# Another order of the prologue's stages in an attention and feed-forward kernel on one core

## The chip, the cores and the metric

The kernel runs on one core of a Trainium2 chip. The core has a matrix engine (PE, TensorE), a vector engine (DVE), an activation engine (ACT), a general engine (POOL) and a sequencer that issues transfers (SP). Each executes its own instructions in order, and they wait for each other by semaphores. Transfers run on 16 DMA engines that all queues share. The metric is the time of one execution on the device in microseconds (us).

## The reference

Attention with two kinds of masks over 8 sequences of 576 tokens and 8 heads of 64, then a layer norm and a two-layer network (512 to 2048 to 512) with a residual:

```python
scores = scale * np.matmul(q, k.transpose(0, 1, 3, 2))
mask_local = (rel >= 0) & (rel < 32)                          # heads 0 to 3
mask_strided = (rel >= 0) & (pos[None, :] % 32 == pos[:, None] % 32)   # heads 4 to 7
scores = np.where(masks, scores, -1e9)
attn = np.exp(scores - np.max(scores, axis=-1, keepdims=True))
attn = attn / (np.sum(attn, axis=-1, keepdims=True) + 1e-09)
x = np.matmul(attn, v)                # heads side by side: (8, 576, 512)
xn = (x - mu) / np.sqrt(var + 1e-06) * g_ln
out = x + np.maximum(xn @ w_ch1, 0.0) @ w_ch2
```

## The kernel before

**Tiling.** Two heads make a *pair*; there are 32 pairs, four for each sequence, in the order strided, local, strided, local (heads 4 and 5, 0 and 1, 6 and 7, 2 and 3). The tokens of all sequences are cut into nine chunks of 512. For each chunk the network runs 16 steps, one for each 128 of the 2048 hidden units. The matrices of the network are each split in two parts of a rounded 32-bit format (high and low), and so are the inputs, so that a step takes 24 products of 128x128 by 128x512: eight of the high part of the first matrix (`ffn1_high`, L697), four of its low part (`ffn1_low`, L704), and twelve for the second layer (L724).

**Two regimes.** From chunk 1 on, the pieces of the attention for the next chunk stand at fixed places between the steps. Before that there is a prologue and chunk 0: the pairs 0 to 3 (sequence 0) must be through before chunk 0 can begin, pairs 4 to 8 are worked on between its steps, and the weights of each step come from HBM once and are split into their parts beside it. All of this is written as one list of words, `ORDER`. The program issues the words one after the other, and every engine keeps that order among its own instructions.

**The words.** `T:k:i:buf` turns the rows of q (i=0) or k (i=1) of pair k on PE, and `c:k:i` copies them on ACT. `S`, `mask`, `max`, `sub`, `exp`, `PP`, `pt`, `V`, `den`, `xo`, `X`, `xh`, `xl` carry pair k through scores (PE), mask and maximum (DVE), subtraction (POOL), exponential (ACT), turn (PE), copy (ACT), product with v (PE), division (DVE, two words), turn (PE), and the two parts of x (ACT, DVE). `vs` copies v once more on POOL (local pairs 1 and 3). `r` and `v` load a later pair, `st` stores a pair's result to DRAM (all SP); `tp` turns a loaded pair on DVE, out of a single buffer, so that the next `r` waits for it. For step f: `W:f` loads its two matrices of 512 KB (SP); for each matrix i, `low` (DVE) or `lowA` (ACT), `sc` (ACT), `mg` and `sg` (DVE) rebuild the numbers; `byg`, `add` (POOL), `cm` (PE), `cen` (DVE) multiply by the norm's weights and centre the first matrix; `hi` (ACT, L284) and `lo` (POOL, L288) write the two parts. `F:f`, `H:f`, `hh:f`, `hl:f`, `G:f` are the high and low products of the first layer (PE), the two parts of its result (ACT, DVE) and the second layer of step f (PE). `xr` reads a residual row block from DRAM (SP) and `xs` takes its mean and variance (DVE, POOL).

**Buffers that tie words together.** The last number of a PE word is one of three PSUM buffers; a word that writes a buffer waits until everything that reads the one before it is done. Buffers 1 and 2 become the second layer's sums with `G:0`, and after that only buffer 0 is left. The first layer has one buffer: `F:f` waits for `hl:f-1`. The numbers of one matrix pass through one PSUM buffer as well: `sc` of the next waits for `sg`. `W:10` takes memory that the pairs of sequence 0 used and so waits for `st:0` to `st:3`.

**Where chunk 0 ends.** `G:15` is issued inside chunk 1's first step, behind `ffn1(1, 0)`.

Of the kernel before, what the change touches and what calls it, by code (L numbers as in the profile page):

```python
# [17 lines left out]


ORDER = """  # L20
T:0:0:0 T:0:1:1 c:0:0: T:1:1:2 c:0:1: S:0::0 c:1:1: T:2:0:1 mask:0 max:0 T:1:0:2 c:2:0: sub:0
T:3:1:0 c:1:0: exp:0 S:1::1 PP:0::2 c:3:1: mask:1 pt:0 T:2:1:0 max:1 sub:1 V:0::1 c:2:1: T:3:0:2
den:0 vs:1 exp:1 xo:0 S:2::0 c:3:0: W:0 X:0::1 mask:2 vs:3 PP:1::2 xh:0 max:2 S:3::0 pt:1 xl:0
sub:2 r:4 V:1::2 mask:3 exp:2 low:0:0 sc:0:0 PP:2::1 max:3 pt:2 den:1 sub:3 mg:0:0 V:2::0 W:1 xo:1
exp:3 sg:0:0 X:1::1 tp:4 PP:3::2 sc:0:1 byg:0 xh:1 add:0 pt:3 v:5 V:3::2 den:2 low:0:1 low:1:0 W:2
mg:0:1 xo:2 low:1:1 cm:0::0 sg:0:1 cen:0 hi:0:1 v:4 xl:1 sc:1:0 S:4::0 lo:0:1 hi:0:0 den:3 mg:1:0
X:2::1 lowA:2:1 lo:0:0 mask:4 xh:2 W:3 sg:1:0 lowA:2:0 max:4 byg:1 sc:1:1 xo:3 sub:4 mg:1:1 X:3::0
add:1 xl:2 st:3 exp:4 xh:3 PP:4::2 W:4 sg:1:1 cm:1::1 lowA:3:0 xl:3 sc:2:0 cen:1 F:0 pt:4 mg:2:0
hi:1:0 sg:2:0 hi:1:1 lo:1:0 st:0 V:4::0 sc:2:1 lowA:3:1 H:0 mg:2:1 W:5 byg:2 lowA:4:0 den:4 lo:1:1
sg:2:1 hh:0 lowA:4:1 xo:4 add:2 sc:3:0 hl:0 X:4::0 hi:2:1 v:6 mg:3:0 F:1 xh:4 lo:2:1 sg:3:0  # L30
lowA:5:0 byg:3 xl:4 H:1 sc:3:1 st:2 G:0 lowA:5:1 mg:3:1 hh:1 sg:3:1 st:1 hl:1 sc:4:0 hi:3:1 r:5
mg:4:0 cm:2::0 lo:3:1 cen:2 sg:4:0 hi:2:0 add:3 sc:4:1 F:2 mg:4:1 lo:2:0 sg:4:1 W:6 cm:3::0 byg:4
cen:3 sc:5:0 H:2 hi:4:1 mg:5:0 G:1 add:4 hh:2 tp:5 hi:3:0 lo:4:1 st:4 sg:5:0 lo:3:0 hl:2 sc:5:1
cm:4::0 W:7 cen:4 lowA:6:0 F:3 byg:5 mg:5:1 lowA:6:1 hi:4:0 sg:5:1 add:5 S:5::0 sc:6:0 hi:5:1
lo:4:0 mg:6:0 r:6 H:3 mask:5 G:2 hh:3 lo:5:1 sg:6:0 lowA:7:0 hl:3 sc:6:1 byg:6 max:5 lowA:7:1
cm:5::0 mg:6:1 sub:5 W:8 F:4 cen:5 sg:6:1 add:6 hi:5:0 H:4 tp:6 exp:5 lo:5:0 sc:7:0 cm:6::0 G:3
hh:4 W:9 hi:6:1 mg:7:0 lo:6:1 lowA:8:0 hl:4 lowA:8:1 sg:7:0 F:5 cen:6 byg:7 sc:7:1 r:7 hi:6:0
mg:7:1 add:7 PP:5::0 sg:7:1 lowA:9:1 H:5 lo:6:0 sc:8:0 G:4 hh:5 mg:8:0 pt:5 hl:5 W:10 hi:7:1
sg:8:0 lowA:9:0 lo:7:1 cm:7::0 sc:8:1 F:6 tp:7 byg:8 cen:7 r:8 add:8 H:6 mg:8:1 hi:7:0 V:5::0
sg:8:1 hh:6 lo:7:0 lowA:10:0 hl:6 G:5 sc:9:0 den:5 xo:5 hi:8:1 lowA:10:1 lo:8:1 mg:9:0 W:11 sg:9:0  # L40
cm:8::0 F:7 cen:8 sc:9:1 byg:9 hi:8:0 mg:9:1 add:9 S:7::0 sg:9:1 st:5 sc:10:0 lo:8:0 H:7 mask:7
hi:9:1 W:12 G:6 mg:10:0 lowA:11:0 lo:9:1 max:7 hh:7 lowA:11:1 sg:10:0 sub:7 hl:7 sc:10:1 X:5::0
v:7 byg:10 exp:7 mg:10:1 F:8 xh:5 sg:10:1 lowA:12:1 xl:5 W:13 hi:10:1 H:8 sc:11:0 lo:10:1 cm:9::0
G:7 hh:8 cen:9 lowA:12:0 add:10 mg:11:0 hi:9:0 hl:8 W:14 lo:9:0 sg:11:0 cm:10::0 sc:11:1 F:9
cen:10 byg:11 lowA:13:1 mg:11:1 hi:10:0 add:11 sg:11:1 S:6::0 W:15 lowA:13:0 sc:12:0 lo:10:0 H:9
tp:8 hi:11:1 lowA:14:0 G:8 lo:11:1 hh:9 lowA:14:1 hl:9 r:9 mask:6 F:10 lowA:15:1 mg:12:0 lowA:15:0
max:6 cm:11::0 sg:12:0 sub:6 H:10 cen:11 sc:12:1 G:9 byg:12 hh:10 mg:12:1 exp:6 hl:10 add:12
hi:11:0 sg:12:1 tp:9 lo:11:0 sc:13:0 PP:6::0 hi:12:1 F:11 pt:6 mg:13:0 lo:12:1 r:10 sg:13:0
cm:12::0 H:11 sc:13:1 byg:13 cen:12 mg:13:1 V:6::0 hi:12:0 add:13 sg:13:1 hh:11 G:10 den:6 sc:14:0
lo:12:0 xr:0 hl:11 hi:13:1 mg:14:0 lo:13:1 v:8 xo:6 F:12 sg:14:0 xs:0 sc:14:1 byg:14 cm:13::0  # L50
mg:14:1 st:6 H:12 add:14 cen:13 G:11 hh:12 sg:14:1 hi:13:0 hl:12 sc:15:0 lo:13:0 hi:14:1 mg:15:0
cm:14::0 lo:14:1 sg:15:0 xr:1 F:13 cen:14 sc:15:1 byg:15 xr:2 hi:14:0 mg:15:1 PP:7::0 sg:15:1
lo:14:0 H:13 pt:7 xs:1 hi:15:1 X:6::0 add:15 xr:3 xs:2 hh:13 G:12 xh:6 lo:15:1 hl:13 xl:6 F:14
xs:3 cm:15::0 H:14 cen:15 V:7::0 hi:15:0 hh:14 lo:15:0 G:13 v:9 den:7 hl:14 xo:7 st:7 S:8::0 F:15
mask:8 tp:10 X:7::0 H:15 xh:7 max:8 G:14 hh:15 r:11 xl:7 sub:8 hl:15 exp:8 PP:8::0 pt:8
"""
# [904 lines left out]
```

## Time and profile before

| | |
|---|---|
| time, median of 3 runs | 949.44 us (947.91 to 950.6) |
| the profiled execution | 949.26 us, its span 946.7 us |
| PE busy | 915.5 us, 97% of the span |
| PE busy before 47.1 us | 31.3 us |
| PE busy from 59.9 to 165.3 us | 97.06 of 105.4 us |
| granted PE clock, mean | 0.986 |

The profile shows one execution. Times in it count from the span's start. An engine's idle time is put down to what ended it (the releaser); "issue" means that nothing shown ended it. Lines are those of the listing above.

### The profile page before, as it was taken

How to read it: one execution, taken by the hardware profiler on the slowest of the kernel's cores; microseconds unless marked ns; L12 is line 12 of the kernel's file. 1: busy time of each engine (PE TensorE's matmuls, PEld its weight loads, DVE VectorE, ACT ScalarE, POOL GpSimd, SP SyncE). 2: the span in 40 equal slices, each digit the busy share in tenths (PEclk: the TensorE clock that was granted, in tenths of full speed). 3: DMA queues.
4: the chain of work that ended last, by engine and by line, in shares of the span. 5: the costliest groups of instructions: out<-in, count | busy, mean ns of one | idle time of the engine just before them, and what ended most of it. 6: DMA issues, size and time to landing. Idle time of an engine off the chain costs nothing.

```text
span 946.7 us, 18534 instructions
## 1 busy us (share of the span) xinstructions
PE 915.5 (97%) x7840; PEld 755.2 (80%) x7840; DVE 405.8 (43%) x829; ACT 224.0 (24%) x361; POOL 147.5 (16%) x186
## 2 busy tenths in 40 slices
PE   7689889999999999999999999999999999999997
PEld 6567678888888888888888888888888888888886
DVE  3877676433543355334543344345433321122112
ACT  4576553211111111211111211121112111111110
POOL 5577654000100010001000010001000000000000
PEclk9799999999999999999999999999999999999999
DMA  9999953433433243423343344334221121002001
GB/s 188 222 240 220 272 104 73 106 63 72 89 87 64 50 95 60 97 44 84 62 97 62 86 73 97 62 86 74 72 38 49 36 86 38 1 1 89 1 1 44
DMA packets 239425, 80.14 MB, mean 85 GB/s; under 512 B 190064, under 2 KB 232688, under 8 KB 239344
## 3 DMA queue, kind: packets, MB, share of 16 engines
q1 hardware_dynamic: 236128, 77.27, 36.4%
q10 hardware_dynamic: 3216, 1.71, 0.8%
q8 instruction: 61, 1.00, 0.5%
q14 instruction: 20, 0.16, 0.1%
HBM read 59.48 MB, written 19.46 MB: 83 GB/s over the span
## 4 chain that ended last, share of the span: by engine, by line
PE 92%; issue 2%; DVE 2%; DMA 1%; POOL 1%; SPq 1%; ACT 0%; ACTq 0%; DVEq 0%; POOLq 0%
PE po L724 40%; PE ph L697 27%; PE ph L704 13%; PE m L505 2%; PE m L434 2%; PE n L490 1%; PE n L577 1%; DMA rows<-in_k_dram 1%; SPq L340 1%; PE av L505 1%; PE s L434 1%; PE pp L490 1%; PE cm L271 0%; PE t L360 0%; PE px L577 0%
## 5 line engine op out<-in xcount | busy, mean ns | idle before, releaser
L724 PE MATMUL po<-w,hh 128*128 128x512 f32 x1152 | 361.4, 395 | 0.0
L714 DVE SCALAR_TENSOR_TENSOR hl<-ph,hh 128x512 fp32r<-128x512 f32 x144 | 99.4, 690 | 461.5 <-ACT hh L709 461.1
L724 PEld LDWEIGHTS po<-w,hh 128*128 128x128 f32 x1152 | 211.9, 188 | 44.1
L697 PE MATMUL ph<-xh,w 128*128 128x512 f32 x576 | 228.1, 396 | 2.5 <-ACT w L284 1.4
L697 PE MATMUL ph<-xl,w 128*128 128x512 f32 x576 | 226.6, 393 | 0.0
L724 PE MATMUL po<-w,hl 128*128 128x512 f32 x576 | 224.9, 390 | 0.0
L709 ACT ACTIVATE hh<-ph 128x512 fp32r<-128x512 f32 x144 | 86.0, 597 | 489.7 <-PE ph L704 489.5
L704 PE MATMUL ph<-xh,w 128*128 128x512 f32 x576 | 155.4, 391 | 0.0
L697 PEld LDWEIGHTS ph<-xh,w 128*128 128x128 f32 x576 | 109.6, 190 | 25.8 <-ACT w L284 1.6
L697 PEld LDWEIGHTS ph<-xl,w 128*128 128x128 f32 x576 | 109.7, 191 | 22.6
L724 PEld LDWEIGHTS po<-w,hl 128*128 128x128 f32 x576 | 108.1, 188 | 23.2
L704 PEld LDWEIGHTS ph<-xh,w 128*128 128x128 f32 x576 | 107.2, 188 | 22.0
L480 POOL TENSOR_TENSOR sm<-sm,mx 128x648 f32<-128x648 f32 (+1 forms) x32 | 40.6, 1270 | 413.6 <-DVE mx L475 410.0
L674 POOL TENSOR_TENSOR rs<-rs,mhalf 128x1 f32<-128x1 f32 x36 | 19.8, 549 | 339.7 <-DVE rs L673 339.7
L486 ACT ACTIVATE sm<-sm 128x648 f32<-128x648 f32 (+1 forms) x32 | 23.8, 743 | 121.4 <-POOL sm L480 121.4
L288 POOL TENSOR_TENSOR w<-r,w 128x512 fp32r<-128x512 f32 x32 | 41.1, 1291 | 23.4 <-ACT w L284 19.4
L608 DVE TENSOR_TENSOR xl<-n,xh 128x480 fp32r<-128x480 f32 (+2 forms) x36 | 22.7, 660 | 15.5 <-ACT xh L604 15.5
L475 DVE TENSOR_REDUCE mx<-sm 128x12 f32<-128x648 f32 (+1 forms) x32 | 26.2, 820 | 2.5 <-DVE sm L469 0.5
L555 DVE TENSOR_TENSOR xo<-m,den 64x64 f32<-64x64 f32 (+3 forms) x120 | 27.1, 288 | 0.1
L248 DVE SCALAR_TENSOR_TENSOR p<-p,s 128x512 uint32<-128x512 uint32 x32 | 22.3, 696 | 10.5 <-ACT p L234 10.2
L669 DVE BATCH_NORM_STATS2 st<-x 128x6 f32<-128x512 f32 x36 | 24.3, 676 | 3.8 <-DMA x<-xds 3.8
L730 DVE SCALAR_TENSOR_TENSOR x<-po,rs,x 128x512 f32<-128x512 f32 x36 | 24.5, 736 | 3.1 <-PE po L724 2.8
(96 smaller groups left out, 599.7 us busy)
## 6 DMA issues: line engine op xcount, KB each, us to landing
s<-in_moe_w_ch_dram SPq DMA_DIRECT2D x32, 512.0 KB
out_dram<-x SPq DMA_DIRECT2D x32, 256.0 KB
raw<-in_q_dram SPq DMA_DIRECT2D x112, 72.0 KB
raw<-in_k_dram SPq DMA_DIRECT2D x112, 72.0 KB
xds<-xo SPq DMA_DIRECT2D x32, 162.0 KB
v_l<-in_v_dram SPq DMA_DIRECT2D x32, 144.0 KB
xdl<-xo SPq DMA_DIRECT2D x16, 256.0 KB
x<-xdl SPq DMA_DIRECT2D x32, 128.0 KB
```

Source lines behind the costliest of these rows:

```text
L288: nc.gpsimd.tensor_tensor(out=t[:, 1], in0=self.w[i], in1=t[:, 0].bitcast(F32), op=ALU.subtract)
L434: nc.tensor.matmul(o, lhsT, rhs, start=True, stop=True, tile_position=(64 * h, pos))
L475: nc.vector.reduce_max(mx[:, :, 0:nt], sm, axis=AX.X)
L480: nc.gpsimd.tensor_tensor(out=sm, in0=sm, in1=mx[:, :, 0:nt].unsqueeze(3).broadcast_to([P, 2, nt, sm.shape[3]]), op=ALU.subtract)
L505: nc.tensor.matmul(at(h, t)[cols], self.pt[rows, t, cols], self.v[rows, n, 0:w], start=True, stop=True, tile_position=(64 * h, cols.start))
L555: nc.vector.tensor_tensor(out=xo[r, t0:t1, h0:h1].rearrange("p t h d -> p h t d"), in0=av, in1=den[r, h0:h1, t0:t1].unsqueeze(3).broadcast_to(
L697: nc.tensor.matmul(ph, w1h[:, cc], x[:, cc, :], start=(cc == 0 and i == 0), stop=False)
L704: nc.tensor.matmul(ph, w1l[:, cc], xt[c][0][:, cc, :], start=False, stop=(cc == NCC - 1))
L709: nc.scalar.activation(out=hh, in_=ph, func=AF.Relu)
L714: nc.vector.scalar_tensor_tensor(out=hl, in0=ph, scalar=0.0, in1=hh.bitcast(F32), op0=ALU.max, op1=ALU.subtract)
L724: nc.tensor.matmul(po[i], hx[:, cs], w, start=(f == 0 and n == 0), stop=(f == NFC - 1 and n == 2))
L730: nc.vector.scalar_tensor_tensor(out=x, in0=po[i], scalar=rs, in1=x, op0=ALU.mult, op1=ALU.add)
```

## The change

`ORDER` has the same words, with other places and other PSUM buffers, and one word more, `Fb:0`: `F:0` now multiplies the first three pairs' part of x (six products) and `Fb:0` the fourth pair's (two). Every `F` goes over the parts of x in the order of the pairs, no longer by column. `BY_DVE` is empty and `ONCE` is false, so that the branches they stand in do what was done before.

```diff
-T:0:0:0 T:0:1:1 c:0:0: T:1:1:2 c:0:1: S:0::0 c:1:1: T:2:0:1 mask:0 max:0 T:1:0:2 c:2:0: sub:0
-T:3:1:0 c:1:0: exp:0 S:1::1 PP:0::2 c:3:1: mask:1 pt:0 T:2:1:0 max:1 sub:1 V:0::1 c:2:1: T:3:0:2
-den:0 vs:1 exp:1 xo:0 S:2::0 c:3:0: W:0 X:0::1 mask:2 vs:3 PP:1::2 xh:0 max:2 S:3::0 pt:1 xl:0
...
+T:0:1:0 T:0:0:2 c:0:1: T:1:1:1 c:0:0: c:1:1: S:0::0 T:2:1:2 mask:0 max:0 T:1:0:1 c:2:1: sub:0
+T:2:0:0 c:1:0: exp:0 S:1::2 c:2:0: PP:0::1 mask:1 T:3:1:0 pt:0 max:1 V:0::2 c:3:1: sub:1 S:2::1
+vs:3 vs:1 den:0 exp:1 xo:0 W:0 T:3:0:0 mask:2 X:0::2 c:3:0: max:2 PP:1::1 xh:0 sub:2 S:3::0 r:4
+pt:1 xl:0 low:0:0 sc:0:0 low:0:1 exp:2 mg:0:0 sg:0:0 V:1::1 mask:3 byg:0 W:1 PP:2::2 den:1 max:3
...
+BY_DVE = ()
+ONCE = False
+EARLY_F0 = True
...
-    def ffn1_high(c, f):
+    def ffn1_high(c, f, ccs=range(NCC), ph=None):
         xh, xl = xt[c]
-        ph = ps_h.tile([P, CH], F32, tag="h", name=f"ph{c}_{f}")
+        new = ph is None
+        if new:
+            ph = ps_h.tile([P, CH], F32, tag="h", name=f"ph{c}_{f}")
         w1h = w1s[f][:, 0].rearrange("p (c f) -> p c f", c=NCC)
-        for cc in range(NCC):
+        for n, cc in enumerate(ccs):
             for i, x in enumerate((xh, xl)):
                 nc.tensor.matmul(
-                    ph, w1h[:, cc], x[:, cc, :], start=(cc == 0 and i == 0), stop=False)
+                    ph, w1h[:, cc], x[:, cc, :], start=(new and n == 0 and i == 0), stop=False)
         return ph
...
-            p.load_v()
+            p.load_v(once=ONCE)
...
-            ph[k] = ffn1_high(0, k)
+            ccs = [p.h0 // 2 for p in first]
+            ph[k] = ffn1_high(0, k, ccs[0:-1] if EARLY_F0 and k == 0 else ccs)
+        elif op == "Fb":
+            ffn1_high(0, k, [first[-1].h0 // 2], ph[k])
```

The words of some engines, taken out of the two lists, each in its order. SP, all of its words up to the residual:

```
before  W0 r4 W1 v5 W2 v4 W3 st3 W4 st0 W5 v6 st2 st1 r5 W6 st4 W7 r6 W8 W9 r7 W10 r8 W11 st5 W12 v7
        W13 W14 W15 r9 r10 xr0 v8 st6 xr1 xr2 xr3 v9 st7 r11
after   W0 r4 W1 W2 r5 W3 v4 W4 W5 r6 W6 st3 W7 v5 W8 st0 W9 r7 st1 st4 st2 r8 W10 W11 W12 W13 W14
        st5 v6 W15 v8 st6 v7 r9 xr0 xr1 xr2 v9 xr3 r10 st7 r11
```

PE from pair 3's scores to the first second layer, and DVE from pair 0's `xl` to step 0's centring:

```
PE   before  S3 V1 PP2 V2 X1 PP3 V3 cm0 S4 X2 X3 PP4 cm1 F0 V4 H0 X4 F1 H1 G0
PE   after   S3 V1 PP2 V2 PP3 S4 X1 V3 X2 cm0 X3 PP4 F0 cm1 Fb0 H0 V4 S5 cm2 F1 H1 G0
DVE  before  xl0 mask3 low00 max3 den1 mg00 xo1 sg00 tp4 den2 low01 low10 mg01 xo2 low11 sg01 cen0
DVE  after   xl0 low00 low01 mg00 sg00 mask3 den1 max3 xo1 tp4 mg01 den2 sg01 mask4 low10 max4 mg10
             xo2 xl1 den3 xo3 sg10 cen0
```

ACT around step 8, and DVE at the end of the list:

```
ACT  before  hh7 lowA110 lowA111 sc101 exp7 xh5 lowA121 hi101 sc110 hh8 lowA120 hi90 ...
ACT  after   hh7 hi80 hi81 pt6 lowA100 sc100 lowA101 sc101 lowA110 hh8 sc110 hi90 lowA111 lowA121 ...
DVE  before  ... mg140 xo6 sg140 xs0 mg141 cen13 sg141 hl12 ... xs1 xs2 hl13 xl6 xs3 cen15 ... hl15
DVE  after   ... hl14 tp9 sg151 hl15 xl7 xs3 tp10 xs2 xs0 xs1
```

## Rows read from the trace of the kernel before

**Rows 1.** The page: busy time of the engines, and the granted clock.
```profile
PE 915.5 (97%) x7840; PEld 755.2 (80%) x7840; DVE 405.8 (43%) x829; ACT 224.0 (24%) x361; POOL 147.5 (16%) x186
...
PEclk9799999999999999999999999999999999999999
```
**Rows 2.** Windows by stage: length, busy PE, PEld, DVE, ACT, POOL, clock, DMA, GB/s.
```profile
0.00:47.10 47.10, 31.30 (x804) 27.23 (x805) 26.68 (x63) 23.96 (x34) 24.78 (x51) 0.85 0.96 205
...
59.90:165.30 105.40, 97.06 (x862) 77.43 (x861) 74.85 (x124) 55.31 (x94) 68.95 (x73) 0.97 0.73 174
```
**Rows 3.** What PE waited for, 59.9 to 165.3: total us, times, longest.
```profile
PE cm L271 <- POOL bsum L267: 5.4, 2, 2.9
PE ph L697 <- ACT w L284: 1.4, 1, 1.4
PE ph L697 <- DVE hl L714: 1.0, 1, 1.0
```
**Rows 4.** The chain that ended last, 100 to 143: start, us, what.
```profile
103.51 5.69 issue
...
112.58 3.12 PE ph L697 x8
...
126.78 1.85 PE ph L697 x8
...
133.49 5.32 issue
```
**Rows 5.** ACT in order of time, where it meets a weight transfer.
```profile
41.47 0.69 ACT L241 ACTIVATE s<-s 128x512 uint32<-128x512 uint8 x1 [1.58 <-DMA s<-in_moe_w_ch_dram]
...
107.97 0.67 ACT L241 ACTIVATE s<-s 128x512 uint32<-128x512 uint8 x1 [3.73 <-DMA s<-in_moe_w_ch_dram]
```
**Rows 6.** DVE in order of time, at `xs:0`.
```profile
137.66 0.69 DVE L669 BATCH_NORM_STATS2 st<-x 128x6 f32<-128x512 f32 x1 [3.82 <-DMA x<-xds]
```
**Rows 7.** DVE in order of time, at `mask:3` and `tp:4`.
```profile
27.80 0.82 DVE L462 TENSOR_TENSOR sm<-s,mask_l 128x640 f32<-128x640 f32 x1 [2.23 <-PE s L434]
...
31.97 1.25 DVE L409 STREAM_TRANSPOSE qt_s<-raw 128x576 f32<-128x576 f32 x1
```
**Rows 8.** DVE groups of the first 59.9 us: `mg` and `low`.
```profile
L248 DVE SCALAR_TENSOR_TENSOR p<-p,s 128x512 uint32<-128x512 uint32 x9 | 6.2, 694 | 1.8 <-ACT p L234 1.7
...
L244 DVE TENSOR_SCALAR s<-s 128x512 uint32<-128x512 uint32 x4 | 1.5, 388 | 0.0
```
**Rows 9.** Windows: GB/s moved (last column) while known transfers ran.
```profile
24.00:25.00 1.00, 0.45 (x41) 0.28 (x21) 0.94 (x2) 0.97 (x3) 0.94 (x2) 1.00 1.34 218
...
39.00:40.00 1.00, 0.72 (x28) 0.73 (x32) 0.97 (x4) 0.63 (x1) 0.70 (x2) 0.50 0.94 257
...
80.00:84.00 4.00, 3.02 (x15) 2.15 (x14) 2.95 (x5) 1.48 (x3) 1.86 (x3) 1.00 1.07 381
120.00:122.00 2.00, 2.00 (x10) 1.67 (x9) 2.00 (x4) 0.66 (x2) 0.40 (x1) 1.00 0.77 126
```
**Rows 10.** PE in order of time: V3, S4, X3, PP4, F0.
```profile
34.34 0.96 PE L505 MATMUL av<-v_l,pt 64*32 64x65 f32 x70 [0.84 <-ACT pt L495]
37.32 0.45 PE L505 MATMUL av<-v_l,pt 64*32 64x65 f32 x10 [2.03 <-issue]
...
39.28 1.54 PE L434 MATMUL s<-kt_s,qt_s 64*64 64x54 f32 x48 [0.78 <-DVE r L274]
...
43.93 1.09 PE L577 MATMUL px<-ident,xo 128*128 128x128 f32 x4 [1.64 <-DVE xo L555]
45.50 1.54 PE L490 MATMUL pp<-ident,sm 128*128 128x128 f32 x6 [0.48 <-ACT sm L486]
...
47.12 0.77 PE L697 MATMUL ph<-xh,w 128*128 128x512 f32 x1
```
**Rows 11.** PE in order of time: `G:0`, and the first product of chunk 1.
```profile
57.09 0.61 PE L724 MATMUL po<-w,hh 128*128 128x512 f32 x2
...
165.06 0.47 PE L697 MATMUL ph<-xh,w 128*128 128x512 f32 x1
```

More of the change, by code (lines that the diff above doesn't have):

```diff
@@ L20 @@
 ORDER = """
-T:0:0:0 T:0:1:1 c:0:0: T:1:1:2 c:0:1: S:0::0 c:1:1: T:2:0:1 mask:0 max:0 T:1:0:2 c:2:0: sub:0
-T:3:1:0 c:1:0: exp:0 S:1::1 PP:0::2 c:3:1: mask:1 pt:0 T:2:1:0 max:1 sub:1 V:0::1 c:2:1: T:3:0:2
-den:0 vs:1 exp:1 xo:0 S:2::0 c:3:0: W:0 X:0::1 mask:2 vs:3 PP:1::2 xh:0 max:2 S:3::0 pt:1 xl:0
-sub:2 r:4 V:1::2 mask:3 exp:2 low:0:0 sc:0:0 PP:2::1 max:3 pt:2 den:1 sub:3 mg:0:0 V:2::0 W:1 xo:1
-exp:3 sg:0:0 X:1::1 tp:4 PP:3::2 sc:0:1 byg:0 xh:1 add:0 pt:3 v:5 V:3::2 den:2 low:0:1 low:1:0 W:2
@@ L26 @@
[L26 to L55, printed above, removed]
@@ L56 @@
-"""
+T:0:1:0 T:0:0:2 c:0:1: T:1:1:1 c:0:0: c:1:1: S:0::0 T:2:1:2 mask:0 max:0 T:1:0:1 c:2:1: sub:0
+T:2:0:0 c:1:0: exp:0 S:1::2 c:2:0: PP:0::1 mask:1 T:3:1:0 pt:0 max:1 V:0::2 c:3:1: sub:1 S:2::1
+vs:3 vs:1 den:0 exp:1 xo:0 W:0 T:3:0:0 mask:2 X:0::2 c:3:0: max:2 PP:1::1 xh:0 sub:2 S:3::0 r:4
+pt:1 xl:0 low:0:0 sc:0:0 low:0:1 exp:2 mg:0:0 sg:0:0 V:1::1 mask:3 byg:0 W:1 PP:2::2 den:1 max:3
+sc:0:1 pt:2 xo:1 sub:3 V:2::2 tp:4 exp:3 W:2 PP:3::0 mg:0:1 pt:3 S:4::1 add:0 den:2 sg:0:1 r:5
+X:1::0 mask:4 sc:1:0 hi:0:1 low:1:0 V:3::1 max:4 lowA:2:0 xh:1 lo:0:1 mg:1:0 xo:2 sub:4 xl:1 W:3
@@ new lines @@
+exp:4 X:2::2 den:3 xo:3 lowA:2:1 cm:0::0 sg:1:0 xh:2 X:3::1 cen:0 byg:1 xl:2 hi:0:0 PP:4::0 v:4
+sc:1:1 lo:0:0 low:1:1 mg:1:1 xh:3 F:0 pt:4 add:1 sg:1:1 xl:3 sc:2:0 W:4 hi:1:1 lowA:3:1 mg:2:0
+cm:1::0 cen:1 Fb:0 sg:2:0 lowA:3:0 H:0 byg:2 sc:2:1 tp:5 add:2 W:5 V:4::0 hh:0 hi:1:0 mg:2:1
+S:5::1 lo:1:0 hl:0 sg:2:1 hi:2:1 cm:2::2 lo:1:1 F:1 cen:2 sc:3:0 r:6 mask:5 lowA:4:1 hi:2:0 H:1
+G:0 mg:3:0 sg:3:0 hh:1 den:4 lo:2:0 byg:3 sc:3:1 hl:1 lowA:4:0 W:6 lowA:5:0 mg:3:1 sg:3:1 F:2 H:2
+add:3 xo:4 sc:4:0 hi:3:1 mg:4:0 lowA:5:1 lo:3:1 sg:4:0 cm:3::0 st:3 G:1 cen:3 sc:4:1 byg:4 hi:3:0
@@ new lines @@
+W:7 hh:2 mg:4:1 sg:4:1 hl:2 sc:5:0 X:4::0 lo:3:0 mg:5:0 F:3 H:3 xh:4 sg:5:0 lo:2:1 add:4 v:5 xl:4
+byg:5 hi:4:1 sc:5:1 mg:5:1 lowA:6:0 cm:4::0 G:2 add:5 cen:4 hh:3 sg:5:1 hi:4:0 hl:3 sc:6:0 lo:4:0
+max:5 W:8 hi:5:1 cm:5::0 lowA:6:1 lowA:7:1 mg:6:0 sub:5 cen:5 sg:6:0 exp:5 F:4 H:4 tp:6 byg:6
+PP:5::0 st:0 hh:4 G:3 pt:5 add:6 W:9 hl:4 hi:5:0 sc:6:1 lo:4:1 lowA:7:0 mg:6:1 cm:6::0 lo:5:0
+sg:6:1 F:5 cen:6 sc:7:0 r:7 hi:6:0 mg:7:0 S:6::0 lowA:8:0 lo:6:0 sg:7:0 H:5 mask:6 sc:7:1 byg:7
+add:7 G:4 mg:7:1 hh:5 lowA:8:1 sg:7:1 hl:5 sc:8:0 st:1 lo:5:1 max:6 lowA:9:0 cm:7::0 mg:8:0 st:4
@@ new lines @@
+st:2 sub:6 cen:7 tp:7 hi:7:0 F:6 H:6 lo:7:0 V:5::0 hh:6 sg:8:0 r:8 hl:6 hi:7:1 sc:8:1 byg:8 G:5
+lowA:9:1 den:5 add:8 exp:6 mg:8:1 sg:8:1 sc:9:0 xo:5 F:7 hi:6:1 mg:9:0 lo:6:1 lo:7:1 W:10 sg:9:0
+cm:8::0 H:7 cen:8 sc:9:1 mg:9:1 PP:6::0 hh:7 G:6 sg:9:1 hi:8:0 hi:8:1 hl:7 lo:8:0 byg:9 pt:6 tp:8
+lo:8:1 lowA:10:0 F:8 sc:10:0 add:9 lowA:10:1 mg:10:0 W:11 W:12 S:8::0 sg:10:0 sc:10:1 H:8 mask:8
+byg:10 lowA:11:0 mg:10:1 cm:9::0 hh:8 G:7 add:10 sg:10:1 cen:9 sc:11:0 hl:8 hi:9:0 lowA:11:1
+lo:9:0 cm:10::0 F:9 lowA:12:1 mg:11:0 sg:11:0 cen:10 sc:11:1 byg:11 W:13 W:14 lowA:12:0 hi:10:0
@@ new lines @@
+S:7::0 mg:11:1 sg:11:1 add:11 H:9 mask:7 sc:12:0 lo:10:0 G:8 hi:9:1 mg:12:0 sg:12:0 hh:9 hl:9
+sc:12:1 byg:12 lowA:13:0 cm:11::0 mg:12:1 F:10 add:12 lowA:14:1 cen:11 st:5 v:6 sg:12:1 lo:9:1
+cm:12::0 sc:13:0 W:15 H:10 cen:12 hi:11:0 max:7 X:5::0 hi:10:1 G:9 mg:13:0 xh:5 lo:10:1 hh:10
+hi:11:1 sg:13:0 xl:5 lo:11:0 lowA:14:0 hl:10 V:6::0 hi:12:1 lowA:13:1 F:11 lo:12:1 v:8 den:6
+sc:13:1 xo:6 byg:13 lo:11:1 X:6::0 mg:13:1 sg:13:1 add:13 H:11 xh:6 st:6 G:10 sc:14:0 xl:6 hh:11
+v:7 sub:7 hi:12:0 hl:11 cm:13::0 lo:12:0 exp:7 F:12 cen:13 hi:13:1 hi:13:0 lowA:15:0 lo:13:1
@@ new lines @@
+mg:14:0 sg:14:0 byg:14 H:12 PP:7::0 r:9 max:8 sub:8 sc:14:1 mg:14:1 G:11 sg:14:1 lo:13:0 pt:7
+hh:12 hl:12 lowA:15:1 V:7::0 xr:0 exp:8 sc:15:0 add:14 mg:15:0 F:13 den:7 xo:7 sg:15:0 H:13 xr:1
+hh:13 byg:15 cm:14::0 add:15 G:12 cen:14 hi:14:0 sc:15:1 lo:14:0 xr:2 hi:14:1 hl:13 PP:8::0
+mg:15:1 F:14 pt:8 lo:14:1 v:9 cm:15::0 H:14 cen:15 G:13 hi:15:0 hh:14 hl:14 lo:15:0 tp:9 sg:15:1
+F:15 xr:3 H:15 X:7::0 hh:15 hi:15:1 hl:15 r:10 st:7 xh:7 lo:15:1 xl:7 xs:3 G:14 tp:10 xs:2 xs:0
+r:11 xs:1
+"""
+BY_DVE = ()
@@ L752 @@
     for p in first:
-        p.load_rows(0, nc.sync)
-        p.load_rows(1, nc.scalar)
+        if p.k in BY_DVE:
+            p.load_qk(early.tile([P, 2 * S], F32, name=f"raw{p.id}"))
+        else:
+            p.load_rows(0, nc.sync)
+            p.load_rows(1, nc.scalar)
     nc.scalar.dma_start(gcol, g_ln.rearrange("(c p) -> p c", p=P))
```

## The prediction

> **What bounds the kernel now.** I read the page first: PE is busy 915.5 of 946.7 us, so nothing but PE's idle time and its clock can be won, and the granted clock is below full only at the left end of the line [rows 1]. The windows by stage say where: 15.8 us of idle in the first 47.1 us at a mean clock of 0.85, and 8.3 us between 59.9 and 165.3 [rows 2]. Behind that PE has no gap. So the change is judged by two times alone: the start of `G:0`, and the first product of chunk 1, at 57.09 and 165.06 [rows 11]. Next I read what PE waited for in the second stretch: 5.4 us in two waits of `cm` for POOL, and two small ones of 1.4 and 1.0 [rows 3]. The releaser named there is not the cause. The chain shows before each of the two long waits a hole of over 5 us in which no engine of the chain worked [rows 4]; the engines' own rows fill them. At 107.97 ACT ends a wait of 3.73 us for a weight transfer (`lowA:12:1`), with `hi` and `hh` words behind it, for which POOL and then `cm` wait [rows 5]. At 137.66 DVE ends a wait of 3.82 us for a residual row block (`xs:0`), with `sg:14:0` and so `byg` and `cm` behind it in time [rows 6]. After each the clock is low for a while: the eight products of an `F` take 3.12 us where they take 1.85 at full speed [rows 4].
>
> **First stage, up to `F:0`.** Here I follow two engines.
>
> *DVE up to `tp:4`.* Before, DVE is idle 2.23 us until `mask:3` at 27.80, and then works without a break to `tp:4` at 31.97 [rows 7]. Four weight words of step 0 (`low`, `low`, `mg`, `sg`) now stand ahead of `mask:3`: 2 x 0.39 and, with `sg` taken like `mg`, 2 x 0.69 [rows 8], 2.2 us in all, which just fit the idle time. But `low:0:1` waits in order for W0's second matrix. The rate of a weight transfer is 381 GB/s and that of the small pieces of `r` 126 [rows 9]; the 218 of 24 to 25 us is then a mixture with 0.36 of the weights in it, so W0's last byte moved at 24.4. How long until DVE may use it? W2's last bytes moved at about 40.0, where the rate falls from 257, and ACT's wait for it ended at 41.47 [rows 5, 9]: 1.4 us. So `low:0:1` runs at 25.8, `mg` and `sg` end at 27.5, and `mask:3` starts there. Of the 4.17 us that follow, two `mg`/`sg` (1.4) and one `low` (0.4) have gone ahead, yet `max:3`, `den:1` and `xo:1` keep their order, and the two last wait for V1, which waits for the same fetch pause of PE as before; I count the work as 2.9 instead of 2.4 for that. `tp:4` starts at 30.4, 1.6 us earlier. Bounds: 2.2 us (no wait for W0) and 0 (W0 usable only at 27.4, 3 us after its last byte).
>
> The Trainium skill, page "DMA: Bandwidth & Descriptors", section "Anatomy of one DMA", puts the fixed cost of a transfer at about 2.0 us, most of it the confirmation of the last write, for transfers issued on POOL's path. SP's transfer above shows 1.4. By the page's figure `low:0:1` would run 0.6 us later and the sum below would be 9.5 instead of 10.1.
>
> *PE from V3 to `F:0`.* Before, V3 ends at 37.77 (with a fetch pause of 2.03 us in it) and `F:0` starts at 47.12: 9.35 us [rows 10]. In them lie S4 (0.78 wait, 1.54 work), waits of 1.64 before X3 and 0.48 before PP4, and `cm:1`. S4 now goes ahead, into buffer 1, and does not wait for `cen:0` any more: `tp:4` takes two transposes of 1.25, so S4 runs at 32.9 to 34.5. V3 needs its buffer, so `mask:4`; ahead of that DVE has `mg:0:1`, `den:2`, `sg:0:1`, which end at 34.6, and `mask:4` at 35.4. V3 begins at 35.4 instead of 34.34 and, with the same pause (the words ahead of it hold as many products as before, but for S4, X1 and `cm`), ends at 38.9. Behind it X2 1.5, `cm:0` 0.6, X3 1.1, PP4 1.5 at the low clock [rows 10] make 4.8: `F:0` at 43.7. X3 needs `xo:3`: DVE has seven words from 35.4 on, at 0.4 to 1.0 us each, and is there at about 40.2, before PE is. `xl:3` no longer holds `F:0`, as only `Fb:0` needs it. From `F:0` to `G:0` I take the 9.97 us of before [rows 10, 11]: S5 (1 us) comes in, X4 with its wait goes out. **Gain 3.4 us**, bounds 0 (DVE at its late bound, and the pause twice as long) and 5.5 (pause gone).
>
> The first words of the list (k before q, pair 2 before pair 3) I cost at nothing: S0 needs both copies of pair 0 in either order. `Fb:0` is two of the same eight products; the other order over x, `BY_DVE` and `ONCE` change no work.
>
> **Second stage, `G:0` to chunk 1.** PE's work is the same (X4 in, S5 out, 0.2 us). What can go is 8.3 us of idle [rows 2] and the slow clock behind the two long waits, twice 3.12 - 1.85, 2.5 us [rows 4].
>
> *The wait at `xs:0`.* All `xs` now stand behind `hl:15`, with no weight word behind them. The 2.5 us of PE's wait and the 1.3 of clock go. What is late next: `tp:10` and three `xs`, then chunk 1's first `hl`. `tp:10` waits for `r:10`, which now waits for `tp:9`; 0.59 MB at 126 GB/s are 4.7 us, and 1.4. From `tp:9`, about 9 us before chunk 1 (F15, H15, X7, G14 and part of G13), `r:10` lands 3 us before chunk 1 begins, `tp:10` and `xs` take 6: they end 3 us into it, where `hl` is due in 3.4 and only missed after another 4.7 (the pieces of pair 8 and `G:15` stand ahead of the next `F`). Covered.
>
> *The wait for W12.* Ahead of W12 the queue now lacks v6 (0.3 MB, 2.4 us) and st5 (0.32 MB, 0.9 to 2.6 us) [rows 9]: it lands at 103 to 104.7 instead of 107.97. `lowA:12:1` now stands behind `F:9` and behind `hh:8`. `F:9` ran at 112.2 before; less the 3.4 and the 2.9 of this very wait it runs at 105.9, and at 103 if the small waits go too. So the margin is between +2 and -1.7. I charge 1.2 us.
>
> W6 to W9 come earlier (v5, v6 and st0 to st2 stand behind them, r6 ahead: some 6 us at the rates of rows 9), W10 2.3 us later (r8 ahead of it, v6 no more).
>
> *Small waits.* 1.4, 1.0 and 0.5 (the rest of 8.3) belong to `hi`, to `hl` and to fetching; in a list as dense I expect as many again: 2.9 stay. DVE, busy 74.85 of 105.4 us [rows 2], would be at 79% of 95: not a bound, but no slack for many waits.
>
> **Sum**: 3.4 + 8.3 + 2.5 - 1.2 - 2.9 = **10.1 us**. The profiled execution took 949.26 us, within 0.02% of the median 949.44, so 939.2.
>
> **Rivals.**
>
> *The new wait* (22%): one of the long waits lives on at another place. W10 to W14 stand in one block behind `r:8`, which waits for `tp:7` and so for `r:7` to land; ACT meets them at `lowA:10:0`, `11:0`, `12:1`, with `hh:8`, `hi:9:0`, `hi:10:0` behind. For it: the queue moves 174 GB/s over the whole stretch [rows 2], between the rates of its two kinds, so it is hardly ever empty. Against it: the place of `lowA:12:1`. One episode costs what it did before, 2.9 and 1.3 us less the 1.2 charged: 942 to 945.
>
> *No small waits either* (10%): 10.1 + 2.9 + 1.2, 935.
>
> *Given back* (9%): the prologue's lead is lost to fetch pauses or to W0, and the seam to chunk 1 takes the rest: DVE ends `xs` not 3 but 15 us into chunk 1 because `r:10` lands late. Then 949. Against it: `r:10` has nothing big ahead of it.
>
> *Slower* (10%): the block W10 to W14 late as a whole. ACT then waits in order at each of its five places, and each is an episode of 2.9 + 1.3 = 4.2 us. Three eat the gain (12.6 against 10.1); from the fourth on the kernel is slower by more than 0.3%: 939.2 - 1.2 + 4 x 4.2 = 954.8. For it: `r:8` is issued only when DVE has done `tp:7`, in order behind `cen:7` and so behind PE. Against it: `tp:7` stands before `F:6`, some 13 us before `lowA:10:0`, and `r:8` with W10 takes 7.5.
>
> **Chances.** Likeliest 49%, its own range 936 to 942. 0.3% (2.8 us) is about what a measurement of this kernel can tell from no change. Faster: 49 + 22 + 10 and a point of the given back, 82%; the same 8%; slower 10%. The range runs from 932.5 (no waits, the fetch pause gone) to 947.5, which leaves out most of the two last rivals.
>
> **What would show it.** Right: `G:0` near 53.7 and chunk 1 near 155; ACT's waits for weights short; no wait of DVE for x before `hl:15`; clock full from `G:0` on; the rest of the span equal. Wrong: `mask:3` not before 27.8, a wait of `F` or `cm` over 2 us, or `hl` of chunk 1 held by `tp:10`.

## The result, and the profile after

The changed kernel takes **935.7 us**, the median of 4 runs (933.98 to 937.52), the kernel before 950.02 beside it (4 runs, 947.91 to 953.22): a ratio of 0.9847, with a 95% interval of 0.981 to 0.9883. The forecast was 939.2 in a range from 932.5 to 947.5. The profiled execution took 933.98 us, its span is 932.1.

The two times by which the change was to be judged cut the span into three stages. In the first row stands what [rows 1, 2, 11] give, with the span:

| | `G:0` | `G:0` to chunk 1 | chunk 1 to the end | span |
|---|---|---|---|---|
| before | 57.09 | 107.97 | 781.64 | 946.7 |
| after | 54.49 | 94.46 | 783.15 | 932.1 |
| won | 2.6 | 13.5 | -1.5 | 14.6 |
| forecast | 3.4 | 6.7 | 0 | 10.1 |

The page of the kernel after, the lines of [rows 1]:

```profile
PE 910.5 (98%) x7840; PEld 752.3 (81%) x7840; DVE 409.6 (44%) x829; ACT 223.3 (24%) x361; POOL 148.0 (16%) x186
...
PEclk9799999999999999999999999999999999999999
```

Its windows by stage (length, busy PE, PEld, DVE, ACT, POOL, clock, DMA, GB/s), which answer to [rows 2]:

```profile
0.00:54.50 54.50, 40.28 (x959) 34.29 (x960) 37.47 (x76) 29.74 (x44) 29.83 (x57) 0.87 0.94 214
54.50:148.95 94.45, 94.45 (x798) 76.67 (x796) 72.99 (x115) 60.32 (x103) 69.25 (x71) 1.00 0.82 201
148.95:932.10 783.15, 775.73 (x6087) 641.32 (x6085) 299.15 (x639) 133.25 (x214) 48.95 (x59) 1.00 0.29 63
```

The same windows of the kernel before, cut at its own times:

```profile
0.00:57.10 57.10, 40.32 (x883) 34.14 (x884) 34.48 (x76) 32.35 (x49) 31.53 (x58) 0.85 0.95 216
57.10:165.10 108.00, 99.67 (x874) 79.56 (x872) 77.51 (x129) 57.46 (x98) 69.19 (x74) 0.97 0.73 175
165.10:946.70 781.60, 775.56 (x6088) 641.52 (x6086) 293.81 (x626) 134.16 (x215) 46.76 (x55) 1.00 0.29 63
```

The middle rows hold the result. PE is busy for 94.45 us of 94.45: it waits for nothing in the whole second stage, where it had 8.33 us of idle time. Its granted clock is 1.00 in the mean (0.97 before) and its busy time is itself 5.2 us shorter. About 0.5 us of that is work that crossed the cut and is no gain: S5 (0.97 us) and `cm:2` (0.14) now stand ahead of `G:0`, X4 (0.58) behind it. Like for like the first stage won 3.1 us and the second 13.0. The products that change most are those of `F`, which stand behind the waits of before (groups of PE in the second stage, by line; count, busy us and mean ns of one, idle time before them), before:

```profile
L697 PE MATMUL ph<-xh,w 128*128 128x512 f32 x57 | 25.0, 439 | 2.5 <-ACT w L284 1.4 <-DVE hl L714 1.0
L697 PE MATMUL ph<-xl,w 128*128 128x512 f32 x56 | 23.5, 419 | 0.0
```

and after:

```profile
L704 PE MATMUL ph<-xh,w 128*128 128x512 f32 x57 | 23.2, 407 | 0.0
L704 PE MATMUL ph<-xl,w 128*128 128x512 f32 x56 | 21.9, 391 | 0.0
```

As many products take 3.4 us less. PE in order of time, at `F:0`, `G:0`, chunk 1's first product and the one wait behind it:

```profile
43.80 0.78 PE L704 MATMUL ph<-xh,w 128*128 128x512 f32 x1
...
54.49 0.61 PE L731 MATMUL po<-w,hh 128*128 128x512 f32 x2
...
148.95 0.39 PE L704 MATMUL ph<-xh,w 128*128 128x512 f32 x1
...
160.65 0.70 PE L731 MATMUL po<-w,hh 128*128 128x512 f32 x2 [1.41 <-DVE x L737]
```

What ACT waited for in the second stage (us in total, times, longest), its weight words and its `hh` words, before and then after:

```profile
ACT s L241 <- DMA s<-in_moe_w_ch_dram: 13.7, 10, 3.7
...
ACT hh L709 <- PE ph L704: 4.3, 5, 2.1
```
```profile
ACT hh L716 <- PE ph L711: 13.3, 9, 4.6
...
ACT s L246 <- issue: 0.8, 1, 0.8
```

ACT's idle time has changed its owner. Before, it waited ten times for a weight transfer, and its work was late; now its longest total is for PE, and no wait is put down to a weight (one of 0.8 us at a weight word has no releaser that the profile shows). An engine that waits for the one that sets the end has time in hand. ACT's waits for DVE's `r` fell as well, from 21.1 us to 12.7.

### The profile page after: what moved, and what is told of

It is laid out like the page before. It is cut to its first block, busy times and chain, and to the rows that moved or that the text cites. A ratio compares the mean times of both kernels' runs of the same rounds, so it can differ in the third digit from the quotient of the medians.

```text
span 932.1 us, 18549 instructions
## 1 busy us (share of the span) xinstructions
PE 910.5 (98%) x7840; PEld 752.3 (81%) x7840; DVE 409.6 (44%) x829; ACT 223.3 (24%) x361; POOL 148.0 (16%) x186
## 4 chain that ended last, share of the span: by engine, by line
PE 94%; DVE 2%; issue 1%; POOL 1%; DMA 1%; ACT 0%; SPq 0%; DVEq 0%; POOLq 0%; ACTq 0%
PE po L731 42%; PE ph L704 28%; PE ph L711 14%; PE m L510 2%; PE m L439 2%; PE n L495 1%; PE n L582 1%; PE t L365 1%; PE s L439 1%; DMA rows<-in_k_dram 1%; SPq L345 0%; PE pp L495 0%; POOL sm L485 0%; PE av L510 0%; PE cm L276 0%
## 5 line engine op out<-in xcount | busy, mean ns | idle before, releaser
L737 DVE SCALAR_TENSOR_TENSOR x<-po,rs,x 128x512 f32<-128x512 f32 x36 | 24.6, 740 | 3.1 <-PE po L731 2.8
```

What stands on the lines that cost most here:

```text
L737: nc.vector.scalar_tensor_tensor(out=x, in0=po[i], scalar=rs, in1=x, op0=ALU.mult, op1=ALU.add)
```

## Experiments

Times of one profiled execution stand with every kernel, cut at the same two points; that execution is the slowest run of y1, y3 and y7 and the fastest of x2. (The 97.3 us that the expectations of y4, y5 and y6 name for the second stage, and the 105 of x5, are counted 2.8 us further, to the end of chunk 1's first `F` and `H`.) Two things are read off this table before any single row: the second stage is 94.4 to 94.6 us in seven kernels with the new order, and the first stage moves by 4.1 us between two kernels whose words before `G:0` are the same (the changed kernel and y1). The kernel before stood at 950.02 beside the changed kernel (4 runs) but at 947.81 to 948.91 in the three larger groups of the table (53 runs), so that the gain is probably nearer 12 to 13 us than the 14.3 between those two medians.

| kernel | `G:0` | `G:0` to chunk 1 | rest | median us (runs) | before beside it | ratio, 95% interval |
|---|---|---|---|---|---|---|
| x1_xs_last | 58.31 | 106.01 | 781.88 | 946.14 (10) | 948.91 | 0.9965, 0.9949 to 0.9981 |
| x2_lowA12_late | 58.69 | 103.09 | 781.82 | 948.68 (10) | 948.91 | 0.9999, 0.9982 to 1.0016 |
| x3_both | 57.27 | 102.39 | 781.84 | 945.0 (8) | 948.91 | 0.9962, 0.9936 to 0.9988 |
| x4_v6_st5_late | 56.94 | 106.04 | 781.62 | 946.31 (10) | 948.91 | 0.9972, 0.995 to 0.9993 |
| x5_sp_and_both | 55.31 | 103.35 | 782.24 | 943.73 (10) | 947.81 | 0.9967, 0.9944 to 0.9991 |
| y1_xs_early | 58.60 | 94.53 | 781.87 | 934.1 (4) | 947.81 | 0.9869, 0.9843 to 0.9895 |
| y2_lowA | 56.00 | 94.62 | 783.48 | 936.63 (4) | 947.81 | 0.9892, 0.987 to 0.9914 |
| y3_both | 59.42 | 94.42 | 781.56 | 935.38 (4) | 947.81 | 0.9875, 0.9852 to 0.9898 |
| y4_whole_F0 | 56.94 | 94.53 | 783.13 | 936.72 (6) | 948.5 | 0.9879, 0.9854 to 0.9904 |
| y5_S4_late | 56.00 | 94.51 | 783.49 | 936.86 (6) | 948.5 | 0.9881, 0.9857 to 0.9906 |
| y6_sp_back | 60.63 | 95.26 | 783.11 | 940.56 (6) | 948.5 | 0.9924, 0.9898 to 0.9951 |
| y7_v4_xs_early | 58.56 | 94.47 | 781.57 | 935.78 (6) | 948.5 | 0.9867, 0.9839 to 0.9895 |

### The two long waits, one at a time, in the kernel before

The forecast put most of the second stage's gain on two causes. Each was removed alone, then both.

x1: the residual's statistics at the end of the list.

```diff
-... sg:14:0 xs:0 sc:14:1 ... pt:7 xs:1 hi:15:1 ... xr:3 xs:2 hh:13 ... F:14 xs:3 cm:15::0 ... pt:8
+... sg:14:0 sc:14:1 ... pt:7 hi:15:1 ... xr:3 hh:13 ... F:14 cm:15::0 ... pt:8 xs:0 xs:1 xs:2 xs:3
```

> The kernel before, with only the four xs words (statistics of the residual rows, DVE and POOL) moved behind hl:15. My theory: DVE's wait of 3.8 us for x was the cause of the second long wait of cm (2.5 us) and of one slow F (1.3 us): the PE wait near 141.8 is gone, chunk 1's first product comes 3.8 us earlier, about 946 us. Rival: sg:14 and the words behind it wait for something else as well (the tile that lo must free, or the weights), so that cm still waits there and the time stays within 1 us of 949.4.

The wait of `cm` at `xs:0` went, the other one stayed (2.54 us at 115.39), and the stage became 2.0 us shorter, not 3.8; two small waits were longer (2.07 us at an `F` for `hi` instead of 1.44, 1.16 at a `cm` instead of 0.40); the median fell by 2.8.

x2: ACT meets W12's first matrix later.

```diff
-... sg:10:1 lowA:12:1 xl:5 ... cen:9 lowA:12:0 add:10 ... sc:11:1 F:9 ...
+... sg:10:1 xl:5 ... cen:9 add:10 ... sc:11:1 lowA:12:1 lowA:12:0 F:9 ...
```

> The kernel before, with only lowA:12:1 and lowA:12:0 moved on ACT from ahead of hh:8 to behind sc:11:1; the transfers keep their order. My theory: the first long wait of cm came from ACT's place in order, not from the transfer as such: the wait of 2.9 us near 111.8 and the slow F behind it go, chunk 1 begins 4.2 us earlier, about 945 us. Rival: the SP order is what counted; ACT waits for W12 at the new place just as long, PE waits one step later and the time stays within 1 us of 949.4.

The wait of `cm` for W12 went, and `F` waited 2.27 us for `hl` in its place, at 118.60, one step later as the rival had it. The profiled execution shows a stage 4.9 us shorter, but it is the shortest of ten, and their median shows nothing.

x3: both edits.

> The kernel before with both moves (xs behind hl:15, lowA:12 behind sc:11:1). My theory: the two add up, 8.0 us at chunk 1's first product, about 941 us; the rest up to the changed kernel (2.6 us of the first stage, small waits) stays. Rival: the waits move to the next late transfer, so that less than 5 us come.

With both causes gone the stage is 5.6 us shorter, of the 13.5 that the whole change won, and the median 3.9: the rival's "less than 5". PE still waits 5.8 us in it: 2.31 and 0.98 for `hl`, 1.44 for `hi`, 1.04 without a releaser. The chain shows the longest of them (start, us, what):

```profile
108.18 6.18 DMA s<-in_moe_w_ch_dram
...
114.39 0.68 ACT s L243
...
117.75 0.48 ACT hh L711
...
118.26 0.70 DVE hl L716
...
119.00 2.14 PE ph L699 x8
```

The late transfer now holds the next word that needs a weight, ACT's queue behind it holds `hh`, and PE waits 2.31 us at `F`. Here a wait that was taken from one word of an in-order queue passed to the next.

x4: two transfers behind all weights, on SP alone.

```diff
-... hi:2:1 v:6 mg:3:0 ... sg:9:1 st:5 sc:10:0 ... W:15 lowA:13:0 ...
+... hi:2:1 mg:3:0 ... sg:9:1 sc:10:0 ... W:15 st:5 v:6 lowA:13:0 ...
```

> The kernel before with only two transfers moved on SP: v:6 and st:5 behind W:15, so that W6 and later weights are issued earlier. My theory: v:6 blocked SP until V4 was done, so W6 to W9 come 2 to 4 us earlier and W12 about 4 us earlier (103 to 105 instead of 107.97); the wait of cm near 111.8 shrinks to under 1 us and about 4 us are won. Rival: the DMA engines are full anyway and W12 comes less than 2 us earlier, so that at most 2 us are won.

The stage is 1.9 us shorter and the median 2.6, between the 4 of the theory and the 2 of its rival; `cm` still waits 1.70 us at 108.92, and about 3 us for `xs:0`.

x5: x3, with `v:5` behind `W:7` and `v:7`, `st:5`, `v:6` behind `W:15`.

> The kernel before with both earlier moves (xs behind hl:15, lowA:12 behind sc:11:1) and four transfers moved back on SP: v:5 behind W:7, and v:7, st:5, v:6 behind W:15. My theory: the waits that stayed when the two words were moved all come from weights that land late, so with the weights earlier PE's idle time between G:0 and chunk 1 falls from 5.8 to under 2 us, and that stage from 105 to about 101 us; 939 to 941 us. Rival: the stage is held by the density of the ACT and DVE words (hl behind hh, r behind tp), and 4 us or more of idle stay; 944 to 945 us.

The stage is no shorter than that of x3 (103.35), and 4.8 us of PE's idle time stay in it, as the rival had it. PE waits 3.21 us at 82.30 for `hl`. DVE in order of time shows why (`tp:6`, behind which `mg` and `hl` stand):

```profile
77.61 1.26 DVE L411 STREAM_TRANSPOSE qt_s<-raw 128x576 f32<-128x576 f32 x1 [2.94 <-DMA raw<-in_q_dram]
79.81 1.26 DVE L411 STREAM_TRANSPOSE kt_s<-raw 128x576 f32<-128x576 f32 x1 [0.95 <-DMA raw<-in_k_dram]
```

What was late is the load of pair 6, `r:6`, with `v:5` now just ahead of it on SP: its transposes ran when they did in x3 (77.68 and 79.53), although `G:0` was 2.0 us earlier. A wait of ACT of 5.00 us for a weight ended at 82.26, but it stood behind `hh`, and `F` did not depend on it. In the first stage `cm` waits 2.8 us for `xo`. So in the old order neither the two named words nor this order of four transfers with them reaches even half of the stage's gain; another order of the transfers was not tried there.

### The order of transfers, put back in the kernel after

```diff
-... W:1 PP:2::2 ... r:6 mask:5 ... add:4 v:5 xl:4 ... W:11 W:12 S:8::0 ... cen:11 st:5 v:6 ... hh:11 v:7 sub:7 ...
+... W:1 v:5 PP:2::2 ... r:6 v:6 mask:5 ... add:4 xl:4 ... W:11 st:5 W:12 v:7 S:8::0 ... cen:11 ... hh:11 sub:7 ...
```

> The changed kernel, but on SP v:5, v:6, st:5 and v:7 stand ahead of the weights again, about where the kernel before has them (v:5 behind W:1, v:6 behind r:6, st:5 behind W:11, v:7 behind W:12). Theory A (the order of transfers is a cause by itself): W12 to W15 land 3 to 6 us later, ACT waits for one or two of them again, and the second stage grows from 97.3 to 100 to 103 us; the time is 3 to 5 us over that of the changed kernel. Theory B (the order of DVE, ACT and POOL is the cause, and the transfers have room in it, as moving them in the kernel before bought only 2 to 4 us): the second stage stays under 99 us, no wait of ACT for a weight transfer over 1 us.

The time is 940.56 us, 3.7 to 4.8 over the three other kernels that ran beside it, and every one of its six runs (939.07 at least) is longer than any of theirs (937.74 at most). Its size is that of the first theory, its place is not; and of the second theory the sign "no wait of ACT for a weight transfer over 1 us" failed. ACT in order of time, at its two longest waits for a weight:

```profile
41.75 0.67 ACT L247 ACTIVATE s<-s 128x512 uint32<-128x512 uint8 x1 [4.66 <-DMA s<-in_moe_w_ch_dram]
42.32 0.57 ACT L610 ACTIVATE xh<-px 128x512 fp32r<-128x512 f32 x1
...
119.67 0.66 ACT L247 ACTIVATE s<-s 128x512 uint32<-128x512 uint8 x1 [3.43 <-DMA s<-in_moe_w_ch_dram]
```

The windows of the second stage, columns as above:

```profile
60.60:155.90 95.30, 94.67 (x798) 76.87 (x797) 72.67 (x115) 59.79 (x103) 67.94 (x70) 1.00 0.76 192
```

At 119.67 ACT waits for a weight nearly as long as it did at the worst place of before (3.73 us, [rows 5]), and PE pays little: the stage is 95.3 us, 0.8 longer. The larger part of the loss is read at 41.75: `v:5` ahead of W2 makes `lowA:2:0` wait, `xh` stands behind it on ACT, `F:0` comes at 47.30 and `G:0` at 60.63. In this order the second stage can take a late weight, and the first stage can't take one of 4.66 us (in y1, 1.78 us at the same word left `F:0` at 43.80).

### Three parts of the first stage, undone

y4: `F:0` in one piece, behind `xl:3`, and no `Fb:0`.

```diff
-... xh:3 F:0 pt:4 add:1 sg:1:1 xl:3 sc:2:0 ... cen:1 Fb:0 sg:2:0 ...
+... xh:3 pt:4 add:1 sg:1:1 xl:3 F:0 sc:2:0 ... cen:1 sg:2:0 ...
-EARLY_F0 = True
+EARLY_F0 = False
```

> The changed kernel, but with F:0 in one piece again: all eight products together behind xl:3, and no Fb:0. It isolates the new word. Theory A (the division matters): the six products ran while PE would otherwise have waited for X3's two parts of x; without it PE waits for xl:3 about 1.5 to 2 us and cm:1 stands behind that, so G:0 comes 1 to 2 us later and the time is 1 to 2 us over that of the changed kernel. Theory B (it does not): cm:1 and other words could have filled the hole just as well, G:0 moves less than 0.7 us and the time less than 0.7 us, which these rounds cannot tell from nothing. The second stage is 97.3 us long by both.

`F:0` started at 45.39 and its last product waited 0.58 us, until DVE's `xl:3` was done. The last product of `Fb:0` in the changed kernel waits 0.28 us for the same word, so the new word saves 0.3 us there. The median is 1.0 over that of the changed kernel, whose ratio's interval it shares: not told apart.

y5: S4 late again, in buffer 0.

```diff
-... pt:3 S:4::1 add:0 ... r:5 X:1::0 mask:4 ... F:0 pt:4 ...
+... pt:3 add:0 ... r:5 X:1::0 ... cen:0 S:4::0 byg:1 xl:2 mask:4 max:4 hi:0:0 sub:4 exp:4 F:0 PP:4::0 ... pt:4 ...
```

> The changed kernel, but S:4 stands behind cen:0 again and takes PSUM buffer 0, as in the kernel before; its mask, maximum, subtraction and exponential follow it, and F:0 stands ahead of PP:4. By the prediction's account S:4 early saved the wait of 0.78 us before it and the 1.64 before X3: then G:0 comes 1.5 to 3 us later and the time is 1.5 to 3 us over that of the changed kernel. Rival: PE had those waits taken by others (X2 waits 1.77 for xo:2 in the changed kernel), so that the early S:4 gains under 1 us at G:0. The second stage is 97.3 us long by both.

`F:0` came at 40.83, since PP4 now stands behind it, and PP4 waited 2.5 us for `sub` and `exp`; `G:0` came at 56.00. The median is 1.2 over the changed kernel's. That S4's place is worth 1.5 us or more isn't shown.

y2: three of step 0's and step 1's `low` words moved from DVE to ACT.

```diff
-... low:0:0 sc:0:0 low:0:1 ... low:1:0 ... low:1:1 ...
+... low:0:0 sc:0:0 lowA:0:1 ... lowA:1:0 ... lowA:1:1 ...
```

> The changed kernel with low:0:1, low:1:0 and low:1:1 on ACT (lowA) in place of DVE. Theory A (two engines in each other's way): these words took 1.3 to 1.5 us on DVE instead of 0.39 because an instruction of POOL ran beside them; on ACT they take 0.7, mask:3 starts 1.1 us earlier (27.0 instead of 28.1) and G:0 starts 1 to 2 us earlier. Theory B (late weights, as in the prediction): W0's second matrix landed only at 26.4; then ACT waits for it at the same time, exp:2 behind it is late, PP2 and V2 move back and G:0 gains less than 0.5 us.

This was to take DVE out of POOL's way (see below). The one `low` word left on DVE still took 1.21 us beside POOL, and `mask:3` started at 29.98, not 27.0; ACT did not wait for W0 either, as the second theory had it. The profiled execution met fetch pauses of PE of 1.61 and 2.06 us, more than the changed kernel's 2.4 in all, and `G:0` came at 56.00; the median is 936.63. Inconclusive: what it may save is smaller than what varies.

### The seam

y1: the last statistics earlier on DVE, among step 15's words.

```diff
-... mg:15:1 F:14 ... cen:15 G:13 ... sg:15:1 F:15 ... G:14 tp:10 xs:2 xs:0 r:11 xs:1
+... mg:15:1 xs:2 F:14 ... cen:15 xs:0 G:13 ... sg:15:1 xs:1 F:15 ... G:14 tp:10 r:11
```

> The changed kernel with three of the four xs words earlier on DVE: xs:2 behind mg:15:1, xs:0 behind cen:15, xs:1 behind sg:15:1, where DVE is idle 2.9, 1.2 and 2.5 us. My theory: the 1.4 us that PE waits at 160.7 for the x of chunk 0 (L737) came from these words standing in front of chunk 1's first hl; the wait goes, 1.4 us less span. Rival: the residual rows land later than these places, DVE waits for them ahead of hl:14 and PE waits 1 us or more near 141 to 147 instead.

The wait at the seam went, and the last stage is 781.87 us long instead of 783.15. No word before `G:0` was touched, yet `G:0` came at 58.60 instead of 54.49. `F:0` starts at 43.80 in both; the 4.1 us arise behind it. PE waits 2.26 us for pair 4's v instead of 0.47, and 0.78 for POOL, and the eight products of `F:1` after these waits take 3.2 us instead of 1.9.

y3: y1 and y2 together.

> The changed kernel with both edits (three xs earlier, low on ACT). If both theories hold, 2.5 to 3.5 us less than the changed kernel, about 932 to 933 us; if neither does, 935.7 within 2 us.

The last stage is 781.56, `G:0` at 59.42, the median 935.38: as the changed kernel.

y7: y1, and `v:4` behind `r:5` instead of behind `W:3`.

```diff
-... sg:0:1 r:5 X:1::0 ... PP:4::0 v:4 sc:1:1 ...
+... sg:0:1 r:5 v:4 X:1::0 ... PP:4::0 sc:1:1 ...
```

> The changed kernel with two repairs: v:4 stands on SP behind r:5 instead of behind W:3, so that V:4 need not wait for pair 4's v (0.5 us in the changed kernel, 2 to 3 in two of its variants), and xs:2, xs:0, xs:1 stand earlier on DVE, so that chunk 1's finish does not wait at the seam (1.4 us). If both waits are real costs, G:0 comes 0.5 to 2 us earlier and the seam gives 1.4: 1.5 to 3 us under the changed kernel. Rival: pair 4's v ahead of W3 makes W3 2 us later, lowA:3 and with it cm:3 wait for it, or the fetch pauses take the lead back: within 1 us of the changed kernel.

V4's wait for pair 4's v (0.47 us in the changed kernel, 2.3 in y1) went as well. But W3 then landed later, as the rival had it: ACT waited 3.13 us for it at 50.92, `hh:0` stands behind that word, and `F:1` waited 2.0 us for `hl:0`. The fetch pauses came to 5.8: `G:0` at 58.56. The last stage is 781.57, the median 935.78. In three kernels the seam's 1.3 to 1.6 us are seen in the profile, and none of their times is distinguishable from that of the changed kernel: the first stage spreads wider. No version is shown to beat it.

## Why the prediction was right, and where it wasn't

**The direction, and the time.** The kernel is faster, within the range and just below the 936 to 942 of the likeliest case. The rival "no small waits either" gave 935, for the right reason in the second stage; that it comes so close is in part luck, since the clock gave more than it counted, and the first stage and the seam less. No long wait lived on elsewhere, and the block from W10 to W14 held nothing. Two of the three signs of being wrong came true, `mask:3` not before 27.8 and chunk 1's first `hl` held behind `tp:10`; what each cost is told below.

**Second stage: the mechanism held, two terms were mis-sized.** 8.3 us of idle were to go, all but 2.9 of small waits and a pinch of 1.2 at W12. Both are 0. The step that failed is the sentence "in a list as dense I expect as many again": density was taken for lack of slack, and the table of ACT's waits shows the reverse, 13.3 us in which ACT is ahead of PE. The slow clock was sized at 2.5 us, from the two `F` behind the long waits; PE's busy time fell by 5.2, some 4.7 without the work that crossed the cut (0.5, where the prediction counted 0.2), and 3.4 of it in the products of `F`. Products behind the small waits and of other words had been slow too.

**Its causes were named too narrowly.** "The wait at `xs:0`" and "the wait for W12" are true of the trace: x1 and x2 each removed the wait that they aimed at. But together they account for 5.6 of 13.5 us (x3), and x5 adds nothing to that. y6 shows that in the second stage four of the transfers need not be where the change puts them either. What is left is the rest of the new order as a whole: the words of PE, DVE, ACT and POOL, and the other transfers (`r`, `st`, W). Which of them do it wasn't tried, and stays open.

**First stage: 3.4 forecast, 2.6 seen, and neither is firm.** `F:0` came at 43.80 where 43.7 was worked out, but not by the steps given. DVE in order of time, which answers to [rows 7], and POOL beside it:

```profile
24.90 1.93 DVE L249 TENSOR_SCALAR s<-s 128x512 uint32<-128x512 uint32 x2
...
28.08 0.82 DVE L467 TENSOR_TENSOR sm<-s,mask_l 128x640 f32<-128x640 f32 x1
...
30.67 1.25 DVE L414 STREAM_TRANSPOSE qt_s<-raw 128x576 f32<-128x576 f32 x1
...
35.88 1.44 DVE L249 TENSOR_SCALAR s<-s 128x512 uint32<-128x512 uint32 x1
```
```profile
25.22 1.33 POOL L485 TENSOR_TENSOR sm<-sm,mx 128x648 f32<-128x648 f32 x1
...
35.75 1.28 POOL L293 TENSOR_TENSOR w<-r,w 128x512 fp32r<-128x512 f32 x1 [3.09 <-ACT w L289]
```

`mask:3` is at 28.08, not 27.5, and later than before. The step that failed is "`low:0:1` waits in order for W0's second matrix": DVE waits for no transfer there. The two `low` words take 1.93 us instead of 0.78, beside POOL's copy and subtraction (see below). V3 (36.03) had no fetch pause in it, where one of 2.03 had been kept, and X2 then waited 1.77 us for `xo:2`, which no step had. So an error of one sign met one of the other, and that `F:0` came out within 0.1 us is luck. From `F:0` to `G:0` the 9.97 us of before were taken over; there are 10.69, and 14.8 in y1. That step left out that `v:4` now stands behind `r:5` and W3 on SP, and V4 waits for it, with a slow clock behind the longer wait (y1).

How firm the difference is can be estimated, since the two later stages hardly vary: the four runs of the changed kernel have spans of 932.1, 932.5, 935.6 and 934.9 us, and less 94.46 and 783.15 their `G:0` is at about 54.5, 54.9, 58.0 and 57.3. With the words of before it stands at 57.09, 58.31, 58.69 and 57.27 (before, x1, x2, x3). The profiled pair is near the favourable end: the four estimates have a mean of 56.2, the four kernels with the old words 57.8, so that 1.7 us is the likelier size (an estimate from these eight).

**The seam: "Covered" was wrong.** The statistics were to end 3 us into chunk 1. `hl` of chunk 1's first step ran at 154.53, 5.6 us into it (its `hh` was done at 152.53) and still in time for the next `F`. What was late was behind it, a word that the step didn't follow: the finish of chunk 0 (L737), which stood on DVE behind the `hl` and the next pairs' division, mask and maximum, began at 159.11, and the second layer's buffers were free 1.41 us late. Loss: 1.5 us of the 14.6.
